# A planned kernel of attention and four layers: transfers modelled as rings, and repeated dry plans

## The chip, the cores and the metric

One core of a Trainium2 chip runs the whole program. The metric is device microseconds of one execution; the kernel before was run three times, with a median of 897.54 us (897.0 to 898.54). Engines: TensorE (PE, with its weight loads PEld), VectorE (DVE), ScalarE (ACT), GpSimd (POOL) and SyncE (SP, which here only issues DMAs).

## The reference

Sigmoid attention over 4 batches of 12 heads, 448 tokens, head size 64, and behind it two feed-forward blocks (1792 tokens, 768 to 2048 to 768), in float32 with float64 weights:

```python
def _attn_ref(q, k, v):
    scores = scale * np.matmul(q, k.transpose(0, 1, 3, 2)) - np.log(S)
    attn = 1.0 / (1.0 + np.exp(-scores))
    return np.matmul(attn, v).astype(np.float32)

def _moe_ref(x, w_in, w_out):
    h = x @ w_in
    g = h - np.tanh(h)
    return (g @ w_out).astype(np.float32)

def _moe2_ref(x, w_in, w_out, alpha):
    h = x @ w_in
    g = np.maximum(h, 0.0) + alpha * np.minimum(h, 0.0)
    return (g @ w_out).astype(np.float32)
```

The result is `_moe2_ref(_moe_ref(attention), ...)`.

## The kernel before

**Two levels.** `body` doesn't issue instructions. It describes them: each call of `plan.add` (line 77) makes a node with the engines that may run it, its cost on each, the function that emits it, the names that it reads and writes, a latency `lat`, and for some a `window`, a `keep` and an `early`. At the end `plan.run()` (line 1037) simulates five queues, T (TensorE), A (ScalarE), V (VectorE), G (GpSimd) and S (SP), and emits each node in the moment in which the simulation starts it. So the order of the instructions on each engine, the engine of a node that may run on A or V, and the SBUF slot (one of 51, `NSLOT`) of each name that begins with "s" all come out of this simulation. On the chip each engine then runs its list in that order, and semaphores hold it where data isn't there yet. TensorE's order is fixed: it is the order of the `add` calls.

**Due times.** `deadlines` (line 104) walks back from the end and gives each node the latest start, `late`, that keeps its successors in time; `early` pulls it forward by hand. `run` (line 111) takes for each free engine the ready node with the smallest `late`. A node with a `window` isn't taken while its `late` lies further than that behind the `late` of TensorE's next node; a node that needs a new slot leaves `keep` slots free unless it is urgent.

**Transfers.** A node with a cost "M" (in MB) is a DMA. The plan of before has one pipe for all queues: `moved` (line 115) is the time at which the pipe is free, and lines 185 to 187 move it on:

```python
if "M" in n.cost:
    moved = max(moved, now + 0.8) + n.cost["M"] * self.MB
    n.end = moved + n.lat
```

`MB` is 1 / 0.36 us per MB. `lat` is set by hand for each kind: 4.0 us for a stage load or a scratch store, 5.0 for an accumulating transfer, 2.2 for a fetch, 1.9 to 4.0 for the first loads of q and k.

**Attention.** Heads go in 24 pairs, two pairs to a group, 12 groups. `load_pair` (line 488) loads q and k of a pair (448 KB) on SP and `split` (line 290) cuts it into two float16 parts: the high part on ScalarE or VectorE, the low one on VectorE. A group has seven units, each 128 keys of a pair by 448 queries for two heads; unit 6 holds the last 64 keys of both pairs. `scores` (line 508) makes six float16 matmuls (three passes, two heads side by side), or twelve for unit 6, into one of three PSUM tiles `ps` in turn, and ScalarE's sigmoid empties it. `values` (line 532) multiplies the sigmoids by v in float32 into `psv`. Three units form a cycle; the values of a cycle follow the scores of the next. `load_first` (line 454) loads pair 0 in two pieces.

**Weights.** Beside all this, 64 units of float64 weights are loaded to four stages (`load_stage`, line 326: the first four on SP, the others on GpSimd), made into float32 by three integer operations of VectorE (`words`, line 332), added up for the seven products of a Strassen scheme (`convert_quarter`, line 362), cut into two float16 parts and stored to a scratch in HBM by GpSimd (`to_scratch`, line 352). `fetch` (line 409, SP) brings them back shortly before use.

**The four layers.** Each is seven products in four quarters for two halves of the tokens, 18 matmuls of 128x128 by 448 for each (`multiply_in`, line 673; `multiply_out`, line 784). The sums of activations are made by `plus` (line 626) and `join` (line 748): on VectorE, or, where `MOVED` is true (layers 0 and 2), by GpSimd's accumulating DMA. `MOVED` is false for layers 1 and 3, the only ones with a `join`. `split_act` (line 312) cuts the sums into float16 parts, on ScalarE or VectorE.

All instructions are issued through one helper, line 218, so the profile's groups are told apart by tiles: `ps<-slot` are scores (64 rows), `ps<-slot,slot` the layers, `psv` the values, `slot<-qk` the loads of q and k.

Of the kernel before, what the change touches and what calls it, by code (L numbers as in the profile page):

```python
# [27 lines left out]
SQK = 2.0 ** 6  # L28
SW2 = 2.0 ** 7
# [10 lines left out]
MOVED = (True, False, True, False)  # L40
KEEP_W, KEEP_F, KEEP_P, WIN_F, WIN_O, WIN_P, SPARE_V, WIN_Q = 9, 4, 2, 16, 36, 30, 7, 55
# [6 lines left out]
PACE = (6, 6)  # L48
PASSES = ((0, 0), (0, 1), (1, 0))
# [15 lines left out]
class Plan:  # L65
# [11 lines left out]
    def add(self, engine, cost, emit, reads=(), writes=(), lat=0.12, window=None, keep=1.0, early=0.0):  # L77
        node = Node(len(self.nodes), engine, cost, emit, reads, writes, lat, window, keep, early)
# [14 lines left out]
        for name in node.touched:  # L93
            if name[0] == "s":
                self.uses[name] = self.uses.get(name, 0) + 1
# [8 lines left out]
    def deadlines(self):  # L104
        total = sum(n.cost["T"] for n in self.nodes if n.engine == "T")
        for n in reversed(self.nodes):
            length = min(n.cost.values())
            ends = [a.late - (0.0 if n.engine == "T" and a.engine == "T" else n.lat) for a in n.after]
            n.late = min(ends, default=total + 8.0) - length - n.cost.get("M", 0.0) * self.MB - n.early

    def run(self, dry=False):
        self.deadlines()
        engines = "TAVGS"
        at = dict.fromkeys(engines, 0.0)
        moved = 0.0
# [8 lines left out]

        for n in self.nodes:
            n.left = len(n.before)
            if not n.left:
                enter(n)
# [3 lines left out]
        while done < len(self.nodes):  # L132
            picked = None
            base = order[turn].late if turn < len(order) else 1e9
            for e in engines:
                if at[e] > now + 1e-9:
                    continue
                if e == "T":
# [34 lines left out]
            e, n = picked  # L173
            begun.add(n)
# [54 lines left out]
MM = 0.1882  # L229
# [3 lines left out]
def body(ctx: ExitStack, tc, qkd, vd, w1, w2, w3, w4, al, out):  # L233
# [92 lines left out]
    def load_stage(i, queue):  # L326
# [3 lines left out]
        add(queue, {queue: 0.06 if queue == "S" else 0.6, "M": 0.786}, f, [], [(f"#stage{i % NSTAGE}",)], lat=4.0)  # L330
# [21 lines left out]
    def to_scratch(key, name, scale, early=0.0):  # L352
# [3 lines left out]
        if DIRECT[key[0]]:  # L356
# [3 lines left out]
            parts(dst, (0,)), [("#scr", key)], lat=4.0, early=early)  # L360

    def convert_quarter(m, q):
# [90 lines left out]

    def load_first():
# [26 lines left out]
        high(S, mid, "A", 0, 1)  # L481
# [3 lines left out]
        high(mid, T2, "A", 1, 2)  # L485
        low(mid, T2, 1, 2)

    def load_pair(i):
# [4 lines left out]
            [], whole(name), window=WIN_Q, keep=8.0, lat=(1.9, 3.0, 4.0, 4.0, 3.7, 3.5)[i] if i < 6 else 2.2)  # L493
# [3 lines left out]
    def load_values(g, c0=0, c1=T2):  # L497
# [6 lines left out]
            window=WIN_Q, keep=8.0, lat=2.7 if first else 3.5 if g < 2 else 2.2)  # L504
# [3 lines left out]
    def scores(g, u, cost):  # L508
        k = ring[0] % 3
        ring[0] += 1  # L510
        p = pst[k]
        pairs = ((2 * g + u // 3, u % 3),) if u < 6 else ((2 * g, 3), (2 * g + 1, 3))

        def f(e):
            for n, (jk, jq) in enumerate(PASSES):
                for i, c in pairs:
                    v = hl(slot(f"st{i}"))
                    for h in range(2):
                        r = slice(64 * h, 64 * h + 64)
                        m = 128 if c < 3 else 64  # L520
                        rows = slice(0, 128) if c < 3 else slice(64 * (i % 2), 64 * (i % 2) + 64)
                        PE.matmul(p[rows, h, 0:S], v[r, jk, S + c * 128:S + c * 128 + m], v[r, jq, 0:S],
                                  start=(n == 0), stop=(n == 2), skip_group_check=True)

        add("T", {"T": cost}, f, [x for i, c in pairs for x in parts(f"st{i}", (0, 1) if i or not c else (0, 1, 2))], banks(k), lat=0.2)
# [557 lines left out]
```

## Time and profile before

| what | value |
|---|---|
| median of 3 runs | 897.54 us (897.0 to 898.54) |
| span of the profiled execution, first to last instruction | 896.4 us |
| TensorE busy | 889.4 us, 99% |
| VectorE busy | 786.1 us, 88% |
| ScalarE busy | 632.9 us, 71% |
| GpSimd busy | 172.9 us, 19% |
| moved by DMA | 216.58 MB, mean 242 GB/s |
| TensorE's granted clock | full speed throughout (2.4 GHz) |

The page has the span and no time of its own around it, so the median stands 1.1 us above the span shown. A busy share is counted by the union of the spans of instructions. Matmuls overlap in the pipeline (a single one shows some 350 ns, and one starts every 190 ns), so a short stop between two matmuls may not show as idle time; the starts of groups of matmuls show it.

### The profile page before, as it was taken

What the parts mean: (1) busy time and instruction counts of PE and PEld (TensorE: products, weight loads), DVE (VectorE), ACT (ScalarE), POOL (GpSimd) and SP (SyncE); (2) the same over time, 40 slices, a digit from 0 to 9 for tenths busy, and PEclk for the clock granted to TensorE, in tenths of its full rate; (3) what the DMA queues carried; (4) which work ended last, traced back from release to release, by engine and by line L of the source; (5) the groups of instructions that cost most, each with busy time, mean ns of one, the idle gap of its engine ahead of it and who ended that gap; (6) DMA issues with size and microseconds to landing.
All of it is one profiled execution on the core that took longest, in us unless ns stands there. A gap on an engine that the chain in (4) does not pass through costs nothing.

```text
span 896.4 us, 13475 instructions
## 1 busy us (share of the span) xinstructions
PE 889.4 (99%) x5001; PEld 439.6 (49%) x5001; DVE 786.1 (88%) x988; ACT 632.9 (71%) x878; POOL 172.9 (19%) x261
## 2 busy tenths in 40 slices
PE   9999999999999999999999999999999999999998
PEld 3333335555555555555555555555555555555554
DVE  6799999999999999999999999999989995783311
ACT  7899999999997988997656566559565664242310
POOL 0012533241222120000042223533222100000000
PEclk9999999999999999999999999999999999999999
DMA  9996999998889785634289578999999744454341
GB/s 345 412 386 204 288 380 384 298 279 272 247 262 275 245 263 180 206 129 158 77 245 347 183 276 286 273 271 318 279 309 292 228 150 136 140 186 133 125 136 62
DMA packets 66338, 216.58 MB, mean 242 GB/s; under 512 B 8288, under 2 KB 17120, under 8 KB 66272
## 3 DMA queue, kind: packets, MB, share of 16 engines
q0 software_dynamic: 28256, 113.46, 41.8%
q1 hardware_dynamic: 37728, 101.95, 32.9%
q8 instruction: 39, 0.64, 0.3%
q10 hardware_dynamic: 288, 0.31, 0.1%
q14 instruction: 27, 0.22, 0.1%
HBM read 143.93 MB, written 49.55 MB: 216 GB/s over the span
## 4 chain that ended last, share of the span: by engine, by line
PE 90%; ACT 5%; DMA 2%; issue 1%; DVE 1%; SPq 0%; ACTq 0%; DVEq 0%
PE ps L218 87%; ACT slot L218 4%; PE psv L218 3%; DMA slot<-qk 2%; DVE slot L218 1%; ACT junk L218 0%; SPq L218 0%; ACTq L218 0%; DVEq L218 0%
## 5 line engine op out<-in xcount | busy, mean ns | idle before, releaser
L218 PE MATMUL ps<-slot,slot 128*128 128x448 f16 x4032 | 763.1, 352 | 0.1
L218 PEld LDWEIGHTS <-slot 128*128 128x128 f16 (+1 forms) x4608 | 418.0, 98 | 410.2 <-issue 24.9
L218 ACT ACTIVATE slot<-slot 128x896 f32<-128x896 f32 (+3 forms) x286 | 252.3, 922 | 51.4 <-DVE slot L218 43.6
L218 ACT ACTIVATE slot<-slot,sc 128x896 f16<-128x896 f32 (+2 forms) x175 | 178.0, 1034 | 112.1 <-PE ps L218 74.8
L218 DVE SCALAR_TENSOR_TENSOR slot<-slot,sc,slot 128x896 f16<-128x896 f32 (+1 forms) x160 | 174.3, 1108 | 40.0 <-ACT slot L218 39.8
L218 DVE TENSOR_TENSOR slot<-slot,slot 128x896 f32<-128x896 f32 (+2 forms) x166 | 169.1, 1040 | 0.4
L218 DVE SCALAR_TENSOR_TENSOR slot<-slot,slot 128x768 f16<-128x768 f32 (+2 forms) x138 | 131.2, 963 | 3.6 <-ACT slot L218 2.6
L218 DVE SCALAR_TENSOR_TENSOR slot<-stage,slot 128x768 int32<-128x768 int32 x128 | 120.1, 951 | 0.2
L218 POOL DMA_DIRECT2D scr<-slot x112 | 70.6, 631 | 215.1 <-DVE slot L218 193.6
L218 POOL DMA_DIRECT2D slot<-slot x74 | 67.3, 945 | 111.6 <-DVE slot L218 65.9
L218 ACT ACTIVATE slot<-ps,sc 128x896 f32<-128x896 f32 (+2 forms) x56 | 46.2, 840 | 56.7 <-PE ps L218 54.3
L218 ACT ACTIVATE slot<-ps,cst 128x896 f32<-128x896 f32 x84 | 83.4, 1190 | 1.5 <-PE ps L218 0.8
L218 PE MATMUL psv<-slot,slot 128*64 128x448 f32 (+1 forms) x384 | 71.5, 553 | 0.0
L218 ACT ACTIVATE slot<-ps 128x896 f32<-128x896 f32 (+1 forms) x64 | 48.6, 768 | 31.0 <-PE ps L218 30.9
L218 DVE SCALAR_TENSOR_TENSOR slot<-ps,sc,slot 128x896 f32<-128x896 f32 (+1 forms) x42 | 39.0, 945 | 31.2 <-PE ps L218 31.1
L218 POOL DMA_DIRECT2D stage<-w x60 | 37.7, 632 | 143.0 <-DVE slot L218 140.1
L218 PE MATMUL ps<-slot 64*128 64x448 f16 (+1 forms) x576 | 55.8, 353 | 2.4 <-ACT slot L218 2.0
L218 DVE TENSOR_SCALAR slot<-slot 128x768 f16<-128x768 f32 (+3 forms) x57 | 32.9, 585 | 11.0 <-DMA slot<-qk 10.4
L218 PEld LDWEIGHTS psv<-slot,slot 128*64 128x64 f32 (+1 forms) x384 | 20.5, 135 | 40.1 <-issue 33.1
L218 DVE COPY_PREDICATED slot<-slot,slot 128x896 f32<-128x896 int32 x32 | 38.2, 1208 | 0.0
L218 DVE TENSOR_SCALAR slot<-stage 128x768 int32<-128x768 int32 x64 | 35.1, 555 | 1.4 <-PE psv L218 1.4
L218 ACT ACTIVATE junk<-slot 128x448 f16<-128x448 f32 (+1 forms) x36 | 27.3, 759 | 4.1 <-DVE slot L218 3.7
(32 smaller groups left out, 179.5 us busy)
## 6 DMA issues: line engine op xcount, KB each, us to landing
slot<-scr SPq DMA_DIRECT2D x196, 384.0 KB, 4.4
stage<-w POOLq DMA_DIRECT2D x60, 768.0 KB, 7.0
scr<-slot POOLq DMA_DIRECT2D x112, 384.0 KB, 6.6
slot<-slot POOLq DMA_DIRECT2D x32, 384.0 KB, 6.9
slot<-qk SPq DMA_DIRECT2D x23, 448.0 KB, 9.4
slot<-slot POOLq DMA_DIRECT2D x42, 224.0 KB, 7.2
out_t<-slot SPq DMA_DIRECT2D x23, 224.0 KB, 2.6
slot<-v SPq DMA_DIRECT2D x11, 448.0 KB, 9.4
```

The source lines that it names most:

```text
L218: return lambda *args, **kw: self.tc.keep_in_program_order(f(*args, **kw))
```

## The change

No line that computes is changed for the settings of this kernel: `THREE` and `RAW` are empty, `MOVED_OUT` names no join, and `FIRST_ON` is ScalarE, as before. (`THREE` would multiply values in three float16 passes, `RAW` would make scores straight from float32, `MOVED_OUT` would move single joins to DMA.) The changed parts are the planner's:

- each queue that issues DMAs has a ring. A transfer can begin 1.7 us (`FIRST`) after its issue; the heads of the rings run side by side, each with a share of the rate by its `packet`; alone, a transfer takes 2.7 us per MB (`FULL`) and ends `lag` + 0.2 us later. At most 8 transfers of a queue are under way (`DEPTH`).
- a node's successors learn its end when the simulated transfer ends, not at its issue.
- `improve` runs up to 30 dry plans. In each it takes TensorE's gaps, follows each back along the latest inputs, and gives up to four (`BLAME`) nodes that were ready over 0.3 us before they began an earlier due time. The plan whose last matmul ends first is kept, and `run` then emits it.
- costs: a matmul 0.1892 us (0.1882), GpSimd's part of an accumulating transfer 0.6 us (0.9), the values of unit 6 0.85 us (0.755), sizes of accumulating transfers 0.82, 0.52 and 0.95 MB (0.77, 0.45, 0.9).

The diff, without what the empty settings would switch on:

```diff
+MOVED_OUT = {1: ((), ()), 3: ((), ())}
...
+THREE = ()
+ROUNDS = 30
+BLAME = 4
+DMA_US = (2.7, 1.7, 0.2)
+RAW = ()
+FIRST_ON = "A"
...
-    def __init__(self, n, engine, cost, emit, reads, writes, lat, window, keep, early):
+    def __init__(self, n, engine, cost, emit, reads, writes, lat, window, keep, early, packet, lag, extra):
         self.n, self.engine, self.cost, self.emit = n, engine, cost, emit
+        self.packet, self.lag, self.extra = packet, lag + DMA_US[2], extra
...
     MB = 1.0 / 0.36
+    FULL = DMA_US[0]
+    FIRST = DMA_US[1]
+    DEPTH = 8
 
     def __init__(self, slots):
         self.nodes, self.last, self.readers = [], {}, {}
-        self.uses, self.where = {}, {}
-        self.free = [(0.0, i, s) for i, s in enumerate(slots)]
+        self.total, self.slots = {}, slots
...
+        for n in self.nodes:
+            n.loose = n.late
+            n.head = n.late if n.engine == "T" else 0.0
+            for b in n.before:
+                length = min(c for e, c in b.cost.items() if e != "M")
+                lat = 0.0 if n.engine == "T" and b.engine == "T" else b.lat
+                n.head = max(n.head, b.head + length + b.cost.get("M", 0.0) * self.MB + lat)
+
+    def shares(self, t):
+        heads = [r[0] for r in self.rings.values() if r and r[0][2] <= t + 1e-9]
+        total = sum(h[0].packet for h in heads)
+        return [(h, h[0].packet / total) for h in heads]
+
+    def next_dma(self, t):
+        times = [r[0][2] for r in self.rings.values() if r and r[0][2] > t + 1e-9]
+        times += [t + max(h[1], 1e-6) / share for h, share in self.shares(t)]
+        return min(times, default=None)
+
+    def flow(self, t, to):
+        landed = []
+        while True:
+            then = self.next_dma(t)
+            stop = to if then is None else min(then, to)
+            for h, share in self.shares(t):
+                h[1] -= (stop - t) * share
+            t = stop
+            for r in self.rings.values():
+                if r and r[0][2] <= t + 1e-9 and r[0][1] <= 1e-5:
+                    landed.append((r.pop(0)[0], t))
+            if then is None or then >= to - 1e-9:
+                return landed
 
...
+        self.uses, self.where = dict(self.total), {}
+        self.free = [(0.0, i, s) for i, s in enumerate(self.slots)]
         engines = "TAVGS"
         at = dict.fromkeys(engines, 0.0)
-        moved = 0.0
+        self.rings = {e: [] for e in engines}
+        begun_dma = {e: [] for e in engines}
...
+        def finished(n):
+            for name in n.touched:
+                if name[0] == "s":
+                    w = self.where[name]
+                    w[0] = max(w[0], n.end)
+                    self.uses[name] -= 1
+                    if not self.uses[name]:
+                        self.free.append((w[0], w[2], w[1]))
+            for a in n.after:
+                a.left -= 1
+                hand = 0.0 if n.engine == "T" and a.engine == "T" else n.end
+                a.ready = max(a.ready, hand)
+                if not a.left:
+                    enter(a)
+
         for n in self.nodes:
-            n.left = len(n.before)
+            n.left, n.ready, n.end = len(n.before), 0.0, None
             if not n.left:
                 enter(n)
...
+                issued = begun_dma[e]
+                full = len(issued) >= self.DEPTH and (issued[-self.DEPTH].end is None or issued[-self.DEPTH].end > now + 1e-9)
...
-                    if n.ready > now + 1e-9 or n in begun:
+                    if n.ready > now + 1e-9 or n in begun or full and "M" in n.cost:
                         continue
                     slack = n.late - base
-                    if n.window is not None and slack > n.window:
+                    if n.window is not None and n.loose - loose > n.window:
                         continue
...
+                times += [x[-self.DEPTH].end for x in begun_dma.values()
+                          if len(x) >= self.DEPTH and x[-self.DEPTH].end is not None]
+                dma = self.next_dma(now)
+                if dma is not None:
+                    times.append(dma)
                 times = [t for t in times if t > now + 1e-9]
                 assert times, "no progress"
-                now = min(times)
+                then = min(times)
+                for n, t in self.flow(now, then):
+                    n.end = t + n.lag
+                    finished(n)
+                now = then
                 continue
...
-            n.end = at[e] + n.lat
-            if "M" in n.cost:
-                moved = max(moved, now + 0.8) + n.cost["M"] * self.MB
-                n.end = moved + n.lat
+            n.begin = now
             if not dry:
                 n.emit(e)
             log.append((now, e, n))
-            for name in n.touched:
-                if name[0] == "s":
-                    w = self.where[name]
-                    w[0] = max(w[0], n.end)
-                    self.uses[name] -= 1
-                    if not self.uses[name]:
-                        self.free.append((w[0], w[2], w[1]))
-            for a in n.after:
-                a.left -= 1
-                hand = 0.0 if e == "T" and a.engine == "T" else n.end
-                a.ready = max(a.ready, hand)
-                if not a.left:
-                    enter(a)
+            if "M" in n.cost:
+                issued.append(n)
+                self.rings[e].append([n, n.cost["M"] * self.FULL + n.extra, now + n.cost[e] + self.FIRST])
+            else:
+                n.end = at[e] + n.lat
+                finished(n)
             if e == "T":
                 turn += 1
             done += 1
+        for n, t in self.flow(now, 1e9):
+            n.end = t + n.lag
         self.log = log
+
+    def improve(self, rounds):
+        best = None
+        for _ in range(rounds):
+            self.run(True)
+            order = [n for _, e, n in self.log if e == "T"]
+            end = order[-1].begin + order[-1].cost["T"]
+            if best is None or end < best[0]:
+                best = end, [n.early for n in self.nodes]
+            t = 0.0
+            for n in order:
+                gap = n.begin - t
+                t = n.begin + n.cost["T"]
+                if gap < 0.1:
+                    continue
+                b, found = n, 0
+                while b.before and found < BLAME:
+                    b = max((x for x in b.before if x.engine != "T"), key=lambda x: x.end, default=None)
+                    if b is None:
+                        break
+                    if b.begin - b.ready > 0.3:
+                        b.early += min(gap + 0.5, b.begin - b.ready)
+                        found += 1
+        for n, early in zip(self.nodes, best[1]):
+            n.early = early
+        return best[0]
 
 
...
-MM = 0.1882
+MM = 0.1892
...
-        add(queue, {queue: 0.06 if queue == "S" else 0.6, "M": 0.786}, f, [], [(f"#stage{i % NSTAGE}",)], lat=4.0)
+        add(queue, {queue: 0.06 if queue == "S" else 0.6, "M": 0.786}, f, [], [(f"#stage{i % NSTAGE}",)], lat=4.0, packet=0.234, lag=1.6)
 
...
-            parts(dst, (0,)), [("#scr", key)], lat=4.0, early=early)
+            parts(dst, (0,)), [("#scr", key)], lat=4.0, early=early, packet=0.234)
...
-                add("G", {"G": 0.9, "M": 0.77},
+                add("G", {"G": 0.6, "M": 0.82},
                     lambda e: G.dma_start(out=slot(out_)[:, 0:UC], in_=slot(a)[:, 0:UC], accum_op=ALU.add),
-                    whole(a), whole(out_), lat=5.0)
+                    whole(a), whole(out_), lat=5.0, packet=0.253, lag=1.3)
...
-                lambda e: SP.dma_start(out=slot(name)[:, c0:c1], in_=qkd[0][:, c0:c1]), [], [(name, k)], lat=1.9)
+                lambda e: SP.dma_start(out=slot(name)[:, c0:c1], in_=qkd[0][:, c0:c1]), [], [(name, k)], lat=1.9,
+                early=9.0 - 3.0 * k, packet=0.08)
...
-            [], whole(name), window=WIN_Q, keep=8.0, lat=(1.9, 3.0, 4.0, 4.0, 3.7, 3.5)[i] if i < 6 else 2.2)
+            [], whole(name), window=WIN_Q, keep=8.0, lat=(1.9, 3.0, 4.0, 4.0, 3.7, 3.5)[i] if i < 6 else 2.2,
+            packet=0.14, extra=1.6 if i == 1 else 0.0)
...
-            add("G", {"G": 0.9, "M": 0.45},
-                lambda e: G.dma_start(out=half(*out_), in_=half(*a), accum_op=ALU.add), [a], [out_], lat=5.0)
+            add("G", {"G": 0.6, "M": 0.52},
+                lambda e: G.dma_start(out=half(*out_), in_=half(*a), accum_op=ALU.add), [a], [out_], lat=5.0,
+                packet=0.16, lag=1.2)
...
-            values(g, u, cost_of(0.755, u, "values"), placed)
+            values(g, u, cost_of(0.58 if (g, u) in THREE else 0.85 if u == 6 else 0.755, u, "values"), placed)
...
+    plan.improve(ROUNDS)
     plan.run()
```

## Rows read from the trace of the kernel before

**Rows 1.** The page's first part: busy us (share of the span) xinstructions of each engine.

```profile
span 896.4 us, 13475 instructions
PE 889.4 (99%) x5001; PEld 439.6 (49%) x5001; DVE 786.1 (88%) x988; ACT 632.9 (71%) x878; POOL 172.9 (19%) x261
```

**Rows 2.** Windows: stretch, its us, busy us of PE, PEld, DVE, ACT, POOL; clock, DMA share, GB/s.

```profile
15.00:45.00 30.00, 30.00 (x242) 10.83 (x240) 23.30 (x29) 26.75 (x36) 1.77 (x3) 1.00 1.03 411
45.00:51.00 6.00, 4.46 (x42) 1.59 (x40) 6.00 (x8) 4.53 (x6) 1.08 (x2) 1.00 1.03 405
51.00:105.00 54.00, 53.96 (x422) 19.36 (x420) 53.05 (x81) 54.00 (x74) 19.46 (x29) 1.00 0.85 274
```

**Rows 3.** The chain that ended last, in order of time: start us, us, what.

```profile
32.48 13.91 DMA slot<-qk
...
129.64 201.01 PE ps L218 x1062
...
334.10 557.47 PE ps L218 x2946
```

**Rows 4.** Timeline 30 to 56 us: start, us, engine, operation, count [idle before it, releaser].

```profile
35.46 0.55 POOL L218 DMA_DIRECT2D scr<-slot  x1 [2.73 <-DVE slot L218]
...
36.31 0.54 POOL L218 DMA_DIRECT2D stage<-w  x1 [0.30 <-DMA slot<-qk]
...
44.48 2.64 PE L218 MATMUL psv<-slot,slot 128*64 128x448 f32 x16
...
46.47 0.95 ACT L218 ACTIVATE slot<-slot 128x896 f16<-128x896 f32 x1 [3.12 <-DMA slot<-qk]
...
48.37 1.64 PE L218 MATMUL ps<-slot 64*64 64x448 f16 x18 [1.25 <-ACT slot L218]
...
50.84 2.48 PE L218 MATMUL psv<-slot,slot 128*64 128x448 f32 x12
```

**Rows 5.** Timeline 0 to 30 us: the start, and the same groups undisturbed.

```profile
9.73 2.00 PE L218 MATMUL ps<-slot 64*128 64x448 f16 x24
...
10.01 0.95 ACT L218 ACTIVATE slot<-slot 128x896 f16<-128x896 f32 x1 [1.24 <-DMA slot<-qk]
...
10.86 5.49 ACT L218 ACTIVATE slot<-ps,cst 128x896 f32<-128x896 f32 x6
...
14.38 2.64 PE L218 MATMUL psv<-slot,slot 128*64 128x448 f32 x16
...
21.16 1.88 PE L218 MATMUL ps<-slot 64*128 64x448 f16 x18
...
22.97 2.64 PE L218 MATMUL psv<-slot,slot 128*64 128x448 f32 x16
...
25.42 1.99 PE L218 MATMUL ps<-slot 64*64 64x448 f16 x24
...
27.34 2.48 PE L218 MATMUL psv<-slot,slot 128*64 128x448 f32 x12
```

**Rows 6.** Waits of the whole span: who waited for whom: total us, times, longest.

```profile
ACT slot L218 <- DMA slot<-qk: 6.5, 4, 3.1
...
PE ps L218 <- ACT slot L218: 2.0, 6, 1.2
```

**Rows 7.** Timeline 103 to 108 us, TensorE.

```profile
105.22 1.36 PE L218 MATMUL ps<-slot 64*128 64x448 f16 x12
...
107.42 0.97 PE L218 MATMUL psv<-slot,slot 128*64 128x448 f32 x4
```

**Rows 8.** GpSimd's DMA instructions from 0 to 130 us: busy us, mean ns | idle before.

```profile
L218 POOL DMA_DIRECT2D slot<-slot x12 | 11.1, 975 | 5.9 <-DVE slot L218 3.8 <-PE psv L218 1.5 <-DMA slot<-slot 0.3
L218 POOL DMA_DIRECT2D stage<-w x17 | 9.8, 577 | 53.7 <-DVE slot L218 51.6 <-DMA stage<-w 1.3 <-DMA slot<-slot 0.5
```

**Rows 9.** DMA issues from 0 to 130 us: count, KB each, median us to landing.

```profile
slot<-slot POOLq DMA_DIRECT2D x12, 224.0 KB, 10.3
...
alpha<-al SPq DMA_DIRECT2D x1, 8.0 KB, 11.7
```

More of the change, by code (lines that the diff above doesn't have):

```diff
@@ L28 @@
 SQK = 2.0 ** 6
+SATT = 2.0 ** 14
 SW2 = 2.0 ** 7
@@ L94, in add @@
             if name[0] == "s":
-                self.uses[name] = self.uses.get(name, 0) + 1
+                self.total[name] = self.total.get(name, 0) + 1
         for b in node.before:
@@ L134, in run @@
             base = order[turn].late if turn < len(order) else 1e9
+            loose = order[turn].loose if turn < len(order) else 1e9
             for e in engines:
@@ L450, in sign_of, with split_of @@
         return 1 if i == j else -1
+    def split_of(i):
+        return any((i // 2, u) not in RAW for u in (3 * (i % 2), 3 * (i % 2) + 1, 3 * (i % 2) + 2, 6))
     def load_first():
@@ L479, in low @@
                 [(name, r), (dst, "h", x)], [(dst, "l", x)])
-        high(S, mid, "A", 0, 1)
+        if not split_of(0):
+            return
+        high(S, mid, FIRST_ON, 0, 1)
         high(0, S, "V", 0, 0)
@@ L503, in load_values, with cut, pick, cut_values @@
             [("table",)] if first else [], [(f"sv{g}", k) for k in range(2) if c0 < (384, T2)[k] and c1 > (0, 384)[k]],
-            window=WIN_Q, keep=8.0, lat=2.7 if first else 3.5 if g < 2 else 2.2)
+            window=WIN_Q, keep=8.0, lat=2.7 if first else 3.5 if g < 2 else 2.2, packet=0.065 if first else 0.14)
+        if c1 == T2:
+            cut_values(g)
+    def cut(dst, src, scale, c0, n, step=0, region=0, keep=1.0):
+        def pick(t):
+            return t[:, c0:c0 + n] if not step else t[:, c0:c0 + 2 * step].rearrange("p (h c) -> p h c", h=2)[:, :, 0:n]
+        split(dst, src, whole(src), scale, lambda t: (pick(hl(t)[:, 0]), pick(hl(t)[:, 1])), pick,
+              n * (2 if step else 1), (region,), keep=keep)
+    def cut_values(g):
+        mine = [u for u in range(7) if (g, u) in THREE]
+        for u in mine:
+            if u == 6:
+                cut(f"sV{g}", f"sv{g}", SQK, 768, 128, 0, u, keep=4.0)
+            else:
+                cut(f"sV{g}", f"sv{g}", SQK, 384 * (u // 3) + 64 * (u % 3), 64, 192, u, keep=4.0)
+        if mine:
+            def scaled(e):
+                x = slot(f"sv{g}")
+                if e == "V":
+                    V.tensor_scalar(x, x, SATT * SQK, None, ALU.mult)
+                else:
+                    A.activation(x, x, AF.Copy, scale=SATT * SQK)
+            add("AV", {"A": act(T2), "V": vec(T2, 0, True)}, scaled, (), whole(f"sv{g}"))
     ring = [0]
@@ L516, in f @@
                 for i, c in pairs:
-                    v = hl(slot(f"st{i}"))
+                    m = 128 if c < 3 else 64
+                    rows = slice(0, 128) if c < 3 else slice(64 * (i % 2), 64 * (i % 2) + 64)
+                    keys = slice(S + c * 128, S + c * 128 + m)
                     for h in range(2):
                         r = slice(64 * h, 64 * h + 64)
-                        m = 128 if c < 3 else 64
-                        rows = slice(0, 128) if c < 3 else slice(64 * (i % 2), 64 * (i % 2) + 64)
-                        PE.matmul(p[rows, h, 0:S], v[r, jk, S + c * 128:S + c * 128 + m], v[r, jq, 0:S],
-                                  start=(n == 0), stop=(n == 2), skip_group_check=True)
-        add("T", {"T": cost}, f, [x for i, c in pairs for x in parts(f"st{i}", (0, 1) if i or not c else (0, 1, 2))], banks(k), lat=0.2)
+                        if raw:
+                            if not n:
+                                x = slot(f"sqk{i}")
+                                PE.matmul(p[rows, h, 0:S], x[r, keys], x[r, 0:S], start=True, stop=True,
+                                          skip_group_check=True)
+                            continue
+                        v = hl(slot(f"st{i}"))
+                        PE.matmul(p[rows, h, 0:S], v[r, jk, keys], v[r, jq, 0:S],
+                                  start=(n == 0), stop=(n == 2), skip_group_check=True)
+        needs = []
+        for i, c in pairs:
+            if raw:
+                needs += whole(f"sqk{i}")[:1 if i == 0 and not c else 2]
+            else:
+                needs += parts(f"st{i}", (0, 1) if i or not c else (0, 1, 2))
+        add("T", {"T": cost}, f, needs, banks(k), lat=0.2)
+        scale = 1.0 / 8.0 if raw else 1.0 / (8.0 * SQK * SQK)
         name = f"sa{g},{u}"
         add("A", {"A": act(T2, True, 1)},
-            lambda e: A.activation(two(slot(name)), full(k), AF.Sigmoid, scale=1.0 / (8.0 * SQK * SQK),
-                                   bias=cst[:, 0:1]),
+            lambda e: A.activation(two(slot(name)), full(k), AF.Sigmoid, scale=scale, bias=cst[:, 0:1]),
             banks(k), whole(name))
+        if (g, u) in THREE:
+            cut(f"sA{g},{u}", name, SATT, 0, T2)
     def values(g, u, cost, placed):
@@ L560, in values @@
         add("A", {"A": act(S, True)},
-            lambda e: A.activation(two(slot(name))[:, i], psv[i][:, 0:S], AF.Copy, scale=float(sign_of(i, b % 2))),
+            lambda e: A.activation(two(slot(name))[:, i], psv[i][:, 0:S], AF.Copy, scale=sign_of(i, b % 2) / (SATT * SQK if any(x[0] == g for x in THREE) else 1.0)),
             [("ps3", i)], [(name, i)])
@@ L947, in cost_of @@
         form = "keys" if u == 6 else kind
-        cost = base + (0.1 if base < 0.7 else 0.15) * (form != last[0])
+        cost = base + (0.1 if kind == "scores" else 0.15) * (form != last[0])
         last[0] = form
```

57 lines of the change are left out of this document (33 added, 24 removed).

## The prediction

> **What bounds the kernel now.** I read the busy table of the page first: TensorE is busy for 889.4 of 896.4 us [rows 1]. The reader is to see that no reordering can gain more than the few microseconds in which TensorE stands. Then I asked where it stands. The chain of waits ends in one unbroken piece of 557.47 us of matmuls, and another of 201.01 us lies before it from 129.64 us on, with 3.4 us between them on ScalarE's name [rows 3]. So after 130 us nothing is to be had. Before it, the windows show the loss: TensorE is busy 4.46 of 6 us between 45 and 51 us, while from 15 to 45 us it has no gap [rows 2]. The list of waits says who ended them: TensorE waited 2.0 us on ScalarE, and ScalarE in its turn stood 6.5 us in four waits for loads of q and k [rows 6]. All of this is in the attention stage.
>
> A busy matmul in this profile covers some of a short stop, so I size stops by the starts of groups, against the same group where nothing stopped it.
>
> The large stop. The sixteen value matmuls that start at 44.48 hand over to scores at 48.37, after 3.89 us [rows 4]; the same pair of groups undisturbed takes 2.45 us (22.97 to 25.42) [rows 5]: 1.44 lost. The 24 score matmuls that follow take 2.47 us (48.37 to 50.84) [rows 4] against 1.92 (25.42 to 27.34) [rows 5]: 0.55. Together **1.99 us**. Its cause is in the same rows: ScalarE stood idle for 3.12 us and then started a split at 46.47 [rows 4], ended by a load of q and k issued at 32.48 and 13.91 us on its way [rows 3]. ScalarE works in order, the sigmoids stood behind that split, and TensorE needs a sigmoid to free one of three PSUM tiles. Of 3.12 us idle, 1.99 reached TensorE: the three tiles hid 1.13 us.
>
> Why did the plan put the split there? Behind the load, at 35.46 and 36.31, GpSimd issued a scratch store and a stage load [rows 4], 0.393 + 0.786 MB. The plan of before moves transfers through one pipe in order of issue, so a later issue costs an earlier one nothing. At the 411 GB/s of that stretch [rows 2] these 1.18 MB are 2.9 us of the same DMA engines, about the 3.12 us that ScalarE stood. That transfers of one queue keep their order shows in alpha: 8 KB took 11.7 us on SP's queue [rows 9].
>
> The start. 42 score matmuls from 9.73 to 14.38 take 4.65 us, against 1.92 + 1.81 (the 18 at 21.16 up to 22.97) undisturbed: **0.92 us** lost [rows 5]. ScalarE idles 1.24 us, splits for 0.95 us from 10.01, and only then begins six sigmoids of 0.915 us each at 10.86 [rows 5]. The first scores are done about 0.6 us after 9.73 (six matmuls in pairs, a third of the 1.81 of eighteen), so without the split the sigmoids could begin near 10.35: 0.5 us of the 0.92 is owed to the split. The other 0.4 is ScalarE's own speed: it needs 0.915 us for what TensorE makes in 0.6, and no order changes that.
>
> One more stop: 18 scores from 105.22 to 107.42 take 2.20 us [rows 7] against 1.81: **0.39**. In all 3.30 us.
>
> **The change, part by part.**
>
> The program's work: the new lists of moved joins, raw scores and threefold values are empty, the split's engine stays ScalarE, the joins of layers 1 and 3 were on VectorE and stay there. No instruction is added or removed, TensorE's order is as it was, and each engine's work is the sum it was: 0. What changes is the order on ScalarE, VectorE, GpSimd and SP, the choice between ScalarE and VectorE for a split, and the slot each name gets.
>
> Transfers as rings: one ring per issuing queue, each in its own order, the heads of the rings sharing the rate by packet size. For the load at 32.48 this lets the GpSimd transfers behind it take their part, so the plan lands it later and the split goes behind the sigmoids or to VectorE. I take the whole 1.99 us: the mechanism that was left out is the one that the row shows. Bounds: nothing gained if ScalarE stands elsewhere, 1.99 if not.
>
> The start's rows get their own constants (first transfer 1.7 us, pair 1 with 1.6 us extra). By the new prices the five loads ahead of that split take 0.80 + 0.44 + 2.84 + 1.24 + 1.24 us plus 0.5 for the values on ScalarE's queue, 2.1 before and 1.1 behind: some 10.3 us after the first issue; in the trace the split starts at 10.01 us of the span, right behind its load [rows 5]. Late rather than early, so the split is not put ahead of the sigmoids: gain 0.5, bounds 0 and 0.92.
>
> Thirty dry plans, each giving earlier due times to what was ready and held up before a gap of TensorE, keep the plan with the earliest last matmul. They see only stops that the plan sees. Of the 0.39 at 105 us I take half, 0.2.
>
> The matmul at 0.1892 instead of 0.1882 us: the trace has 557.47 / 2946 = 0.1892 [rows 3]. Before, the plan ran 1.1 us ahead over the 201 us piece, and no stop came of it there: 0. The last-keys units at 0.85 instead of 0.755 and the cap of eight transfers per queue move plan times only: 0. The early due times of the first two loads move what is already first: 0.
>
> GpSimd's accumulating transfer is priced at 0.6 us of GpSimd, before 0.9; the trace has 975 ns [rows 8]. GpSimd is busy for 172.9 us of the span [rows 1], so its time is covered; what it does to the landing is a rival below.
>
> What the new order costs by itself: between 51 and 105 us ScalarE is busy 54.00 of 54 us and VectorE 53.05 [rows 2], so any order leaves some sigmoid late. The old order left 0.39 + 0.42 there and at the start that no transfer caused; a new one should leave about half of that elsewhere: 0.4 lost, bounds 0 and 1.99 (one more stop like the one at 46 us).
>
> Sum: 1.99 + 0.5 + 0.2 - 0.4 = 2.3 us. The profiled span of 896.4 becomes 894.1. The median of the runs, 897.54, lies 1.1 us above that span, which I take for what lies around it: **895.2 us**.
>
> **The rivals.**
>
> The stop moves. The new plan clears 46 us and the start, and one split or accumulate elsewhere stands ScalarE as long as before, 3.12 us for 1.99 of TensorE: 897.54 - 2.3 + 2.0 = 897.2. For it: the plan's rate is one constant (2.7 us per MB, 370 GB/s) and the trace has 274 to 411 in neighbouring windows [rows 2]. Against: it is too slow for the stretch that stopped, so loads land before their plan there.
>
> The change does nothing. If the best of the dry plans is the first and it orders as before, 897.5. Against: every transfer's time changes, so some order must.
>
> The other side: accumulating transfers. Old plan, alone: 0.8 + 1.25 + 5.0 = 7.05 us to landing. New: 0.6 + 1.7 + 1.4 + 1.4 = 5.1 alone, and with SP's ring always full (share 0.16 of 0.30) 6.3. The twelve of this stage had a median of 10.3 us [rows 9]. A consumer planned at 6.3 stands in front of ScalarE or VectorE for 4.0 us; with 1.13 hidden TensorE loses 2.9. One such eats the gain (897.54 - 2.3 + 2.9 = 898.1), two give 897.54 - 2.3 + 5.8 = **901.0**. It decides from a landing more than 1.1 us behind plan with a sigmoid queued behind it. For it: the 10.3, and the 0.6 against 975 ns. Against: much of 10.3 is waiting behind GpSimd's own transfers, which the ring counts too.
>
> On that 975 ns, against 577 ns for a plain load of the stage beside it [rows 8], the Trainium skill has a rule that speaks against this change (SBUF — State Buffer, section SBUF: two separate sides): VectorE in a two-port mode shuts GpSimd out of the port they share, and GpSimd then cannot write the descriptors of its transfers. The rows agree in that the same engine's issue takes unequal times while VectorE is nearly full; they don't show the lock itself. By that rule a GpSimd transfer would start later still than the new plan holds, by up to one such VectorE instruction (the page gives no length); with 0.6 us for it, an estimate, the two stops would cost 1.2 us more, 902.2.
>
> **How the numbers follow.** Forecast, 895.2: 0.50, its own range 893.9 (all 3.30 us and 0.3 of small change) to 896.3 (1.2 us gained). Stop moves, 897.2: 0.25. Does nothing, 897.5: 0.07. Accumulates, 898.1 to 901 and above: 0.18. About 0.2%, 1.8 us, is what a measurement can tell here: faster means under 895.7, slower over 899.3. The forecast puts 0.43 of its half under 895.7, the moved stop 0.04: faster 0.47. Slower: 0.15 of the accumulates and 0.02 of moved stops that come twice (897.54 - 2.3 + 4.0 = 899.2): 0.17. The rest, 0.36, is no change. The range for 8 in 10 goes from 893.9 to 899.5, which leaves out about 0.04 below and 0.14 above.
>
> **What would show it.** Right: the window that held the stop shows no group of scores behind a ScalarE split that waited for a load of q and k; ScalarE's 6.5 us of waits for those loads falls under 3; TensorE's busy time stays near 889 and the span falls. The six sigmoids of the start begin near 10.35. Wrong: new waits of ScalarE or VectorE for accumulated slots in the list of waits, a stop of TensorE after 130 us, or VectorE with more splits than before in the full stretch. If the gain is under 1 us though the stop at 46 us is gone, the term for the new order's own stops was too small.

## The result: slower by one per cent

The changed kernel takes 907.37 us (904.84 to 907.78), the kernel before beside it 897.79: a ratio of 1.0101, 95% interval 1.009 to 1.0113. The forecast of 895.2, its range and its sign were wrong. The profiled execution is the shortest of the changed kernel's runs, 904.84 us with a span of 903.1; the others had spans of 905.3 to 906.0, so the profile shows 6.7 of the 9.6 us.

The page of the changed kernel, first part, as in [rows 1]:

```profile
span 903.1 us, 13515 instructions
PE 891.1 (99%) x5001; PEld 439.1 (49%) x5001; DVE 789.3 (87%) x990; ACT 630.7 (70%) x876; POOL 174.6 (19%) x261
```

The work is the same, with two operations more on VectorE and two fewer on ScalarE; the standing time grew. Where it grew the windows show, with the columns of [rows 2]. First two of the kernel before, which were not among its rows above:

```profile
130.00:290.00 160.00, 160.00 (x848) 82.75 (x847) 158.91 (x205) 148.40 (x192) 45.02 (x67) 1.00 0.93 292
290.00:450.00 160.00, 159.94 (x846) 82.59 (x845) 158.10 (x185) 134.93 (x189) 12.55 (x19) 1.00 0.56 182
```

The same and the next two of the changed kernel:

```profile
130.00:290.00 160.00, 159.51 (x843) 82.22 (x842) 158.64 (x201) 155.07 (x200) 49.13 (x67) 1.00 0.94 286
290.00:450.00 160.00, 157.53 (x828) 80.69 (x827) 156.03 (x178) 123.33 (x175) 11.80 (x18) 1.00 0.55 178
450.00:600.00 150.00, 148.94 (x788) 76.85 (x786) 147.51 (x195) 87.28 (x136) 51.97 (x78) 1.00 0.86 265
600.00:750.00 150.00, 148.37 (x783) 76.38 (x782) 144.22 (x193) 99.00 (x159) 30.00 (x44) 1.00 0.83 256
```

TensorE, without a break there before but for 0.06 us, now stands in every stage of the four layers. In the attention stage it gained: the layers' first matmul starts at 128.22 us against 129.57 before. So the layers took 6.7 + 1.35, some 8.0 us, longer.

Who ended the waits, whole span, columns as in [rows 6]:

```profile
ACT slot L310 <- DMA scr<-slot: 14.7, 8, 4.7
ACT slot L310 <- DMA slot<-slot: 7.9, 4, 4.0
PE ps L310 <- ACT slot L310: 3.7, 8, 0.9
ACT slot L310 <- DMA slot<-qk: 3.1, 3, 1.4
PE ps L310 <- DVE slot L310: 1.5, 3, 0.8
PE ps L310 <- DMA slot<-scr: 1.2, 1, 1.2
```

Before, ScalarE had waited 0.8 us for a scratch store and not at all for an accumulated slot. A store only reads its slot; ScalarE waits because the plan gives that slot to its next result. One such wait, in the timeline of the changed kernel from 305 us (columns of [rows 4]):

```profile
304.79 5.92 PE L310 MATMUL ps<-slot,slot 128*128 128x448 f16 x29
...
309.31 1.04 ACT L310 ACTIVATE slot<-slot,cst 128x896 f32<-128x896 f32 x1 [4.70 <-DMA scr<-slot]
310.26 0.99 ACT L310 ACTIVATE slot<-ps,sc 128x896 f32<-128x896 f32 x1
...
311.30 13.78 PE L310 MATMUL ps<-slot,slot 128*128 128x448 f16 x72 [0.60 <-ACT slot L310]
```

ScalarE stands 4.70 us in front of a slot that a store still reads; the emptying of a PSUM tile (`slot<-ps`) is queued behind it, and TensorE waits for that tile. Another, from 571 us:

```profile
574.86 0.84 ACT L310 ACTIVATE slot<-slot 128x768 f16<-128x768 f32 x1 [1.62 <-DMA slot<-slot]
...
575.90 0.92 ACT L310 ACTIVATE slot<-ps 128x896 f32<-128x896 f32 x1 [0.20 <-DMA scr<-slot]
...
576.86 0.92 PE L310 MATMUL ps<-slot,slot 128*128 128x448 f16 x4 [0.89 <-ACT slot L310]
```

Here the slot of an accumulating transfer comes first. And a third kind, from 716 us, has no transfer in front of it: TensorE waits for a sum of VectorE, which comes out of a queue without a gap from 715.5 us on:

```profile
723.28 1.08 DVE L310 TENSOR_TENSOR slot<-slot,ps 128x896 f32<-128x896 f32 x1
...
724.42 0.92 PE L310 MATMUL ps<-slot,slot 128*128 128x448 f16 x4 [0.85 <-DVE slot L310]
```

The planner's own figures stand beside the trace: for each of GpSimd's 246 transfers the host code holds how long it expects issue to landing to take. In the kernel before 8 took longer than that, and the median was 2.6 us shorter. In the changed kernel 56 took longer (30 of them stores, 14 accumulates, 12 stage loads), and the median is 1.3 us shorter. In its own simulation the changed plan sees no stop of TensorE after 14 us. By these medians the rings are nearer to the truth; the old single pipe was late by a margin that nobody had named.

### The profile page after: what moved, and what is told of

It reads as the page before. It is cut to its first block, busy times and chain, and to the rows that moved or that the text cites. A ratio compares the mean times of both kernels' runs of the same rounds, so it can differ in the third digit from the quotient of the medians.

```text
span 903.1 us, 13515 instructions
## 1 busy us (share of the span) xinstructions
PE 891.1 (99%) x5001; PEld 439.1 (49%) x5001; DVE 789.3 (87%) x990; ACT 630.7 (70%) x876; POOL 174.6 (19%) x261
## 4 chain that ended last, share of the span: by engine, by line
PE 35%; DVE 24%; DMA 8%; issue 6%; ACT 2%; POOL 1%; DVEq 0%; POOLq 0%; ACTq 0%; SPq 0%
PE ps L310 35%; DVE slot L310 23%; DMA slot<-slot 5%; ACT slot L310 2%; DMA slot<-scr 2%; DMA scr<-slot 1%; POOL stage L310 0%; DVE sc L310 0%; POOL sc L310 0%; ACT junk L310 0%; POOL scr L310 0%; POOL slot L310 0%; DVEq L310 0%; POOLq L310 0%; ACTq L310 0%
## 5 line engine op out<-in xcount | busy, mean ns | idle before, releaser
L310 ACT ACTIVATE slot<-slot 128x896 f32<-128x896 f32 (+4 forms) x289 | 253.4, 910 | 79.2 <-DVE slot L310 54.0
L310 ACT ACTIVATE slot<-slot,sc 128x896 f16<-128x896 f32 (+2 forms) x170 | 169.7, 1018 | 100.5 <-PE ps L310 55.7
L310 POOL DMA_DIRECT2D scr<-slot x112 | 68.7, 620 | 210.5 <-DVE slot L310 181.6
L310 ACT ACTIVATE slot<-ps,cst 128x896 f32<-128x896 f32 x84 | 80.0, 1055 | 1.7 <-DVE slot L310 1.3
```

What stands on the lines that cost most here:

```text
L310: return lambda *args, **kw: self.tc.keep_in_program_order(f(*args, **kw))
```

## The experiments

Each run was timed beside the kernel before. Theories: SLACK, the old matmul price let the plan's TensorE run ahead of the chip (0.001 us by 4032 matmuls, 4.0 us by the end) and planned all else early; LANDING, the plan holds GpSimd's transfers to land (to have all their data in place) too soon; DRY PLANS, the earlier due times do the harm; later CHANCE, one unlucky order.

| run | edit of the changed kernel | median us | ratio to before, 95% |
|---|---|---|---|
| (changed) | none | 907.4 | 1.009 to 1.0113 |
| e1 | matmul at 0.1882 | 903.9 | 1.0055 to 1.0089 |
| e2 | one dry plan | 908.3 | 1.0079 to 1.0135 |
| e3 | GpSimd's landings +2.0 us | 898.4 | 0.9996 to 1.0015 |
| e4 | kernel before, matmul at 0.1892 | 903.1 | 1.0044 to 1.0074 |
| e5 | landings +2.0, matmul at 0.1882 | 896.4 | 0.9977 to 0.9994 |
| e6 | landings +2.0, one dry plan | 900.2 | 1.0019 to 1.0043 |
| e7 | stores +2.0 | 900.9 | 1.0023 to 1.005 |
| e8 | accumulates +2.0 | 904.5 | 1.0064 to 1.0094 |
| e9 | seventeen dry plans | 899.5 | 1.0006 to 1.0024 |
| e10 | landings +1.0 | 900.3 | 1.0016 to 1.0035 |
| e11 | landings +2.0, fetches +1.5 | 897.7 | 0.999 to 1.0008 |
| e12 | landings +1.5, matmul at 0.1882 | 896.9 | 0.9981 to 0.9999 |
| e13, e14, e15 | two, three, five blamed | 903.1, 900.2, 901.9 | 1.0043 to 1.0082, 1.0017 to 1.0039, 1.0029 to 1.0059 |
| e16, e17, e18 | landings +2.0; two, three, five blamed | 897.7, 900.2, 899.5 | 0.9987 to 1.0006, 1.0014 to 1.0033, 1.0008 to 1.0028 |

**e1, the old price of a matmul.**

```diff
-MM = 0.1892
+MM = 0.1882
```

> The changed kernel with one number put back: a matmul is planned at 0.1882 us, as before, not 0.1892. Theory SLACK (the old price let the plan's TensorE run 0.5% ahead of the chip, some 4 us by the end, so that every other engine was planned a little early; the exact price takes this away and small delays of the full VectorE reach TensorE): at least 6 of the 9.6 us come back, 901 or less, and as the attention stage is 2 us better perhaps 896. Theory LANDING (GpSimd's transfers are priced to land 1 to 2 us sooner than by the old plan, and engines stand in front of them): no change, 905 to 909. Theory DRY PLANS (the earlier due times of the thirty rounds fit the plan and not the chip): no change, 905 to 909.

3.5 us came back: more than LANDING or DRY PLANS allow, less than SLACK asked for. Two things are mixed in it. In the profile the layers, from their first matmul to their last, take 765.3 us against 770.8 in the changed kernel, 5.5 less; but they start 3.8 us later, since the attention stage of this order stood more:

```profile
132.01 1.31 PE L310 MATMUL ps<-slot,slot 128*128 128x448 f16 x6
```

**e2, one dry plan.**

```diff
-ROUNDS = 30
+ROUNDS = 1
```

> The changed kernel with one dry plan in place of thirty, so that no due time is made earlier; rings and prices stay. DRY PLANS: at least 6 of the 9.6 us come back, 901 or less. SLACK and LANDING: it stays slow, 904 to 911, since a plan with no slack is as thin without the earlier due times.

908.3: DRY PLANS falls. The earlier due times are not what costs.

**e3, later landings**, of stage loads, scratch stores and the two forms of accumulates (only the end of each line is shown).

```diff
-lat=4.0, packet=0.234, lag=1.6)
+lat=4.0, packet=0.234, lag=3.6)
-lat=4.0, early=early, packet=0.234)
+lat=4.0, early=early, packet=0.234, lag=2.9)
-lat=5.0, packet=0.253, lag=1.3)
+lat=5.0, packet=0.253, lag=3.3)
-lat=5.0, packet=0.16, lag=1.2) 
+lat=5.0, packet=0.16, lag=3.2)
```

> The changed kernel with the lag of all four kinds of GpSimd transfers 2.0 us longer in the plan (stage loads 1.6 to 3.6, scratch stores 0.9 to 2.9, accumulating transfers 1.3 to 3.3 and 1.2 to 3.2). Nothing else. LANDING: the waits of ScalarE for scratch stores and accumulated slots (14.7 and 7.9 us) fall to a few us and at least 6 of the 9.6 us come back, 901 or less. SLACK: a part at most, 902 to 907. DRY PLANS: no change, 905 to 909.

898.4, with the waits of

```profile
PE ps L310 <- DVE slot L310: 1.6, 3, 1.0
ACT slot L310 <- DMA scr<-slot: 1.5, 2, 0.7
PE ps L310 <- ACT slot L310: 1.4, 2, 1.3
```

ScalarE's wait for stores fell from 14.7 to 1.5 us, that for accumulated slots is no longer in the list, and 3 of 246 transfers outlast the plan. As a time the run seemed to give LANDING all of the loss; e9 took that back.

**e4, the kernel before with the new price of a matmul.**

```diff
-MM = 0.1882
+MM = 0.1892
```

> The kernel before with one number changed: a matmul is planned at 0.1892 us. No rings, no dry plans, the old landings. SLACK: it loses without anything else of the change, at least 4 us, 902 or more. LANDING and DRY PLANS: within 2 us of the kernel before, 896 to 900.

5.3 us more than the kernel before, by that number alone. The window from 290 us and two rows of its timeline:

```profile
290.00:450.00 160.00, 155.84 (x821) 79.92 (x820) 157.25 (x179) 127.25 (x178) 10.46 (x17) 1.00 0.55 177
```

```profile
327.02 0.84 ACT L218 ACTIVATE slot<-slot 128x768 f16<-128x768 f32 x1 [3.08 <-DMA scr<-slot]
327.33 17.95 PE L218 MATMUL ps<-slot,slot 128*128 128x448 f16 x93 [0.92 <-DMA slot<-scr]
```

ScalarE in front of a store here too, and TensorE in front of a fetch, though every landing price is the old one. The larger stops come later:

```profile
355.90 0.35 PE L218 MATMUL ps<-slot,slot 128*128 128x448 f16 x1 [0.97 <-ACT slot L218]
...
357.37 2.81 PE L218 MATMUL ps<-slot,slot 128*128 128x448 f16 x14 [1.13 <-DVE slot L218]
...
392.72 7.54 PE L218 MATMUL ps<-slot,slot 128*128 128x448 f16 x39 [1.14 <-DVE slot L218]
```

These three are no surprise to the plan. The simulation in e4's own host code has TensorE stand 0.9, 2.1 and 0.7 us at 336, 355 and 390 us, and the last two are in the same groups of matmuls; with 0.1882 it has no stop there. So most of this loss is an order that is bad by its own reckoning, written by a planner without repeated dry plans. It doesn't show that a lead of the plan was worth 5 us.

**e5 and e12, both margins back.** The edits of e1 and e3 together; e12 with 1.5 us in place of 2.0.

> Both margins put back in the changed kernel: GpSimd's transfers land 2.0 us later in the plan (as in the run with late landings, 898.4) and a matmul is planned at 0.1882 us (as in the run with the old matmul, 903.9). LANDING alone: no better than late landings by itself, 897.5 to 899.5. SLACK as a second cause beside it: the layers, which still lost some 3 us there, run without a stop and the attention stage keeps its gain: 893 to 896, under the kernel before.

> Landings 1.5 us later and a matmul planned at 0.1882 us: the better version (896.4 with 2.0 us) with another amount. Both margins are there, so by LANDING and SLACK together 894.5 to 898.5; over 900 would say that its neighbour was luck.

896.4 and 896.9, both below the kernel before by little (e5 by 1.2 us), with intervals that end under 1. 896.4 lies between the two ranges set for e5, so it decides for neither; e12 is in its range. The windows of e5 from 290 us on:

```profile
290.00:450.00 160.00, 158.90 (x838) 81.79 (x837) 158.82 (x178) 132.30 (x185) 13.73 (x21) 1.00 0.57 181
450.00:600.00 150.00, 150.00 (x795) 77.59 (x793) 148.95 (x200) 88.63 (x136) 51.56 (x77) 1.00 0.85 264
600.00:750.00 150.00, 150.00 (x795) 77.58 (x794) 142.84 (x190) 95.86 (x154) 29.36 (x44) 1.00 0.83 264
```

One us is still lost from 290 to 450; the rest is unbroken, and the layers begin at 126.74 us.

**e6, late landings with one dry plan** (the edits of e2 and e3).

> Late landings (2.0 us) with one dry plan in place of thirty. It shows what the thirty rounds are worth once the landings are late enough. If they earn their place: slower than the same with thirty rounds (898.4) by 2 us or more, 900 to 906. If the earlier due times do harm or nothing: 896 to 899.

900.2, against 897.7 to 900.2 for four orders with thirty. The plan of e6 itself holds 3.6 us of stops of TensorE in the layers, that of e3 0.2. Thirty rounds do no harm and take out stops that the plan can see; that they shorten the time isn't shown by a difference of this size.

**e7 and e8, one kind of transfer alone.** The second line of e3's diff; then the last two.

> The changed kernel with only the scratch stores landing 2.0 us later in the plan; the stage loads and the accumulating transfers keep their new prices. ScalarE waited longest for these stores (14.7 us in the changed kernel, before 0.8). If they are the transfers that matter: most of the way to 898.4, 898 to 902, and that wait falls under 3 us. If the accumulating transfers matter (the rival of the prediction): no change, 905 to 909.

> The counterpart: only the accumulating transfers land 2.0 us later in the plan (1.3 to 3.3 and 1.2 to 3.2); stores and stage loads keep their new prices. If accumulates are what stands in front of ScalarE and VectorE: 898 to 902. If the scratch stores are: 904 to 909, with ScalarE's wait for them still over 10 us.

The waits of e7:

```profile
ACT slot L310 <- DMA slot<-slot: 9.3, 6, 3.7
ACT slot L310 <- DMA scr<-slot: 0.7, 2, 0.5
```

and of e8:

```profile
ACT slot L310 <- DMA scr<-slot: 8.5, 8, 2.3
```

For the store's wait in e8 over 10 us had been expected. Each edit takes away the wait of its own kind and leaves the other. The times, 900.9 and 904.5, seem to point to the stores, but they don't rank the two: orders with neither edit lie between 899.5 and 908.3, and the layers alone take 768.1 us in e7 and 767.3 in e8. The difference is in the attention stage: in e8 the layers start at 130.88 us, in e7 at 127.20.

```profile
130.88 2.44 PE L310 MATMUL ps<-slot,slot 128*128 128x448 f16 x12
```

**e9, a control for chance**, and **e13 to e15** (`BLAME` 2, 3 and 5): other orders by the changed kernel's own prices.

```diff
-ROUNDS = 30
+ROUNDS = 17
```

```diff
-BLAME = 4
+BLAME = 2
```

> A control for chance: the changed kernel with seventeen dry plans in place of thirty, so another plan of the same prices, with as few stops in the plan itself. If the prices cause the loss, another order by the same prices is slow too: 903 to 910. If the 9.6 us belong to one unlucky order: anything, and as likely under 900 as over.

> The changed kernel's prices, another order: two nodes blamed for a gap in place of four. The plan itself sees no stop after the start. CHANCE (the control with seventeen plans came out at 899.5 with these prices, so the changed kernel's 907.4 was one unlucky order): 897 to 901. PRICES (landings too early cost some 6 us whatever the order): 902 to 909.

> The changed kernel's prices, three blamed: a further order. CHANCE: 897 to 901. PRICES: 902 to 909.

> The changed kernel's prices, five blamed: a further order. CHANCE: 897 to 901. PRICES: 902 to 909.

Five orders by the same prices: 899.5, 900.2, 901.9, 903.1 and the changed kernel's 907.4, mean 902.4. e9 stayed under the 903 that was asked of the prices; of the other three one came out in the range for the prices, one in that for chance, one between them. All five are slower than before, and the changed kernel is the worst of them; e2, a sixth order by these prices with one dry plan, was 908.3. So about half of the 9.6 us is what these prices cost (902.4 - 897.8 = 4.6) and the other half (5.0) is this order. The split is rough: the kernel before is one order of its planner too, and no other by its prices was run. Waits don't map to time one to one: e9 has a wait of

```profile
ACT slot L310 <- DMA scr<-slot: 13.3, 8, 3.1
```

and is the fastest of the five. What is queued behind them counts too. e14 loses its time in one stage:

```profile
290.00:450.00 160.00, 154.85 (x817) 79.64 (x815) 155.01 (x175) 125.95 (x176) 10.92 (x17) 1.00 0.52 170
```

**e16 to e18**, other orders by the late landings (e3 with two, three, five blamed).

> GpSimd's landings 2.0 us later in the plan, two nodes blamed: another order by the late prices. PRICES: near the 898.4 of its sibling, 897 to 900.5. CHANCE: as wide as with the changed prices, 898 to 908.

> GpSimd's landings 2.0 us later in the plan, three nodes blamed: a further order by the late prices. PRICES: 897 to 900.5. CHANCE: as wide as with the changed prices, 898 to 908.

> GpSimd's landings 2.0 us later in the plan, five nodes blamed: a further order by the late prices. PRICES: 897 to 900.5. CHANCE: as wide as with the changed prices, 898 to 908.

With e3: 897.7, 898.4, 899.5, 900.2, mean 898.9. Later landings are worth 902.4 - 898.9 = 3.5 us on the mean, or 2.2 without the changed kernel itself; three of the five orders without them are slower than all four with them, two lie among them. In pairs that differ in the landings alone (one dry plan; four, two, five, three blamed) they are worth 8.0, 9.0, 5.4, 2.4 and 0.0 us, and ScalarE's wait for stores is 6.5 to 14.7 us without them and 0.7 to 1.6 with them. That they help is shown; how much is known only to within some us.

The runs of a single order scatter as well. The changed kernel's lie 2.9 us apart, those of e2, e9, e13 and e14 3.5 to 5.8, of e15 2.3; with late landings those of e3, e6, e16 and e18 lie within 0.8, of e17 within 2.6. The old matmul price on top gives 896.4 and 896.9: another 2.3 us on the mean, of two orders against four.

**e10 and e11, amounts.** All four lags +1.0 (2.6, 1.9, 2.3, 2.2); then e3 with the fetch's lag at 2.4 as well.

> GpSimd's landings 1.0 us later in the plan in place of 2.0. LANDING, as an amount: between the changed kernel (907.4) and 2.0 us later (898.4), 900 to 904. If it is a matter of chance which plan comes out, no order by amount: outside of that.

> Late landings (2.0 us) and also the fetches of weights from the scratch on SP landing 1.5 us later in the plan (lag 0.9 to 2.4); a matmul at 0.1892 us. TensorE stood for fetches in several of the runs. If what is left of the loss is one more transfer priced too short: 894 to 897, under the 898.4 of late landings alone. If it is the matmul's price (SLACK): 897.5 to 899.5.

900.3 lies where the amount would put it, and inside the scatter of orders too. 897.7 is no better than the best order without the fetch's edit: that fetches are priced too short isn't shown.

## Why the prediction was wrong

**Right: the attention stage.** The stop at 46 us is gone, as this window of the changed kernel shows against the one from 45 us in [rows 2]:

```profile
25.00:50.00 25.00, 25.00 (x208) 9.13 (x202) 22.48 (x29) 23.00 (x31) 3.11 (x5) 1.00 1.03 410
```

The start, in its timeline, against [rows 5]:

```profile
9.38 2.74 PE L310 MATMUL ps<-slot 64*128 64x448 f16 x30
...
9.48 0.95 ACT L310 ACTIVATE slot<-slot 128x896 f16<-128x896 f32 x1 [1.06 <-DMA slot<-qk]
...
10.34 5.48 ACT L310 ACTIVATE slot<-ps,cst 128x896 f32<-128x896 f32 x6
...
13.85 2.64 PE L310 MATMUL psv<-slot,slot 128*64 128x448 f32 x16
```

The sigmoids begin at 10.34, as forecast, though not for the reason given: the split still stands ahead of them, and everything comes 0.35 to 0.5 us sooner. The scores take 4.47 us (9.38 to 13.85) against 4.65. That the number came out at the start was luck. ScalarE's wait for loads of q and k fell from 6.5 to 3.1 us, forecast under 3. Of the stage's 2.3 us the changed kernel shows 1.35, since one new stop came up:

```profile
99.65 1.01 ACT L310 ACTIVATE slot<-ps,cst 128x896 f32<-128x896 f32 x1 [0.63 <-DVE slot L310]
...
100.71 0.76 PE L310 MATMUL ps<-slot 64*64 64x448 f16 x12 [0.90 <-ACT slot L310]
```

In thirteen of the fourteen further orders by the rings and the exact matmul price the layers start at 126.4 to 127.6 us, 2.0 to 3.2 us sooner than before. In e8 they start at 130.88, and in e1, with the old matmul price, at 132.01, both later than before: the bound of nothing gained, if ScalarE stands elsewhere, was real. For most orders that term was of the right size.

**Wrong: the step from "after 130 us nothing is to be had" to a cost of 0.4 us for the new order.** The sum took what the order costs from the attention stage alone and bounded it by one more stop there, 1.99 us. The layers lost 8.0 us in the changed kernel and 4.6 to 8.4 in the five orders with its prices (767.4 to 771.2 us from the first to the last matmul, before 762.8). A stage without a stop was read as a stage with room. The windows of before said otherwise: VectorE was busy for 158.91 and 158.10 of 160 us there. That nothing stood told that this order held, not that any order would. A full VectorE alone doesn't decide it: in e16 it was busy for 159.40 and 159.27 us in the same windows, and the layers lost 1.5 us. Two of the prediction's own signs of being wrong came: waits for accumulated slots, and stops of TensorE after 130 us.

**Wrong, as far as the runs tell: the matmul's price at 0.** The prediction noted that the old plan ran ahead and that no stop came of it, and left it there. Going from 0.1882 to 0.1892 cost 5.3 us in the kernel before (e4), 3.5 in the changed one (e1 read backwards; 5.5 in the layers), and 2.3 on the mean with late landings. So it did not come out at 0. That the lead of the old plan was a margin is not shown: most of e4's stops stand in its own plan, the second pair is one order against one while orders scatter by several us, and the third is small.

**The rival on the other side named the mechanism, but not its place or its kind.** It had GpSimd's transfers landing behind a plan that now holds them shorter, a consumer standing in front of ScalarE, and 901.0 for two such stops; five orders have a mean of 902.4, which is near in number alone, since the stops counted there are others. It put them in the attention stage and on accumulates alone. They came in the layers, and the longer wait is for scratch stores (14.7 us against 7.9), whose readers hold a slot that the plan has given on. Its chance of 0.18 was too small: the prediction held the rings to be better on the whole because they explained one stop, and didn't ask what else the old, too late landings had covered. The rule of the Trainium skill weighed there (GpSimd shut out of a shared port) was not put to the test. That section of the Trainium skill does give a time for one case, which the prediction missed: some 620 ns alone, some 3100 beside a copy of VectorE. No run here shows it; GpSimd's issue of an accumulate measured 988 ns over the whole changed run, 945 before.

**A slip in the sum.** The 1.1 us between median and span belongs to two different executions. Where a run's own time and span are on record they differ by 1.7 us (904.84 and 903.1), so the span forecast, 894.1, meant 895.8. This changes nothing above.

**Left open.** Which edges of the plan make one order 8 us worse than another by the same prices; how much of the gain of late landings is stores and how much accumulates; whether the kernel before is a lucky order of its planner; what the matmul's price does apart from the order that it happens to give; and whether the 1.2 us of e5 would hold for further orders with both margins, of which only two were run.

## What to carry to other kernels

A planner that writes a fixed order for in-order engines did better here with prices that nearly every transfer keeps (3 of 246 over, e3) than with prices nearer to the median (56 over). When a change makes a model truer, ask which errors of the old one worked as margins, and read an engine that is busy all through a stage as a stage at risk even where nothing stops. Before a slower kernel is put down to a margin that is gone, look whether its own plan already stands there, as that of e4 did. And one kernel from a planner is one draw: vary something that should not matter before a difference of one per cent is given to a cause.

## What the runs showed of the hardware

Nothing of the engines themselves was unexpected. What surprised was how little stood between a clean stage and a bad one: with the same work and the same order on TensorE, eighteen plans of one program (the changed kernel and all runs but e4) lay between 896.4 and 908.3 us, by the order and the slots of the other engines and by which of ScalarE and VectorE made a split.
